# Cosine attention and a low-rank mixer on one core: the second half of batch 0's residual goes through a DMA transpose instead of TensorE

## The chip, the cores and the metric

The kernel runs on one core of one Trainium2 chip. The metric is the time of one execution in device microseconds (us); less is better. Five runs of the kernel before the change gave 579.52 to 582.07 us, with a median of 579.97 us.

## What is computed

There are 8 batches, 12 heads, 448 positions and 64 values per head, so that a position has 768 channels. The mixer adds a low-rank mix over positions and then a two-layer network with 3072 hidden units and a residual:

```python
attn = softmax((q/|q|) @ (k/|k|).T / tau) @ v          # per batch and head
x    = attn with heads side by side                    # 8 x 448 x 768
u    = x + (x.T @ U @ V).T                             # U: 448x32, V: 32x448
out  = u + relu(u @ w_ch1) @ w_ch2                     # 768 -> 3072 -> 768
```

The change concerns the `u +` of the last line, for half of the channels of one batch.

## The kernel before

**The tiles.** Two heads make a pair, so each batch has six pairs, numbered 0 to 47 over the whole kernel; pairs 6 to 11 are batch 1. `u` is kept transposed: `uE` (even batches) and `uO` (odd ones) are tiles of 128 partitions by six blocks of 512 columns, with channels on the partitions and positions along the columns. The mixer's first layer (`steps_m1`, line 513) makes 24 tiles of 128 hidden units, each from six matmuls, one for every block of `u`; ScalarE or VectorE applies the ReLU (lines 517 and 519). The second layer (`steps_m2`, line 540) works by chunks of 128 positions and 384 channels: 24 matmuls add up in one PSUM tile `mp`, whose pool has two buffers. Batch 0 has three chunks for each half of the channels.

**The residual.** The output has positions on the partitions, so `u` must be turned back before it is added. For batch 0 TensorE does this: behind the 24 matmuls of a chunk, three more (line 550) multiply blocks of `uE` by the identity into the same `mp`, and then ScalarE (line 554) or VectorE (line 556) copies `mp` into the output tile `o_sb`. Which of the two takes the copy is decided while the program is built, by running totals of each engine's estimated time (`est.act_first`). For all later batches `turn(b, half)` (line 500) issues one DMA transpose of three blocks of `u` into a tile `ut`, and VectorE reads both `mp` and `ut` and adds them into `o_sb` (line 558). The pool of `ut` has two buffers, one of which is held by the raw matrix V until `place_copies` has read it.

**The order of the work.** Everything is issued in an order written out by hand; each engine works through its own list in order and waits on semaphores. Steps of the mixer of batch b-1 are pulled from a list named `fill` between the attention steps of batch b. `put(n, i, fn)` hooks an extra step behind the i-th attention step of pair n. The stage around the change is that of pairs 10 to 14, some 84 to 125 us into the span, where the second layer of batch 0 ends and the first layer of batch 1 begins. What it issues, in order:

- pair 11: scores of pair 11; then `step_V` for both halves of pair 10 (lines 376, 383) with the divisions on VectorE (lines 394, 395), and the DMA transpose `XT` of pair 10 (`step_XT`, line 461).
- pair 12: scores (lines 331, 324); both halves of `step_V` of pair 11 and its `XT`; `step_A2` (line 469), whose matmuls read the `X` tiles of pairs 10 and 11.
- pair 13: scores; `step_H2` (line 483), after which two VectorE adds (line 488) put together blocks 4 and 5 of `uO` from PSUM and the `XT` tiles of pairs 10 and 11, and one VectorE copy (line 491) takes over the last 64 positions of `uE`; then the rest of `fill` and the start of batch 1's first layer.
- pair 14: `step_S3` (line 343) reads the `qkT` tiles of pairs 14 and 15, which come by DMA transposes (`step_T`, line 315).

**The transfer queue.** Nearly all DMAs are issued by SyncE (SP), in one list: loads of q, k and v (lines 205 to 214), the transposes `qkT`, `XT` and `ut`, and the stores of `o_sb` (lines 564, 568). A DMA in that list waits, if need be, for the data that it reads and for the DMA eight places ahead of it in the list, whose semaphore it shares. The second layer's weights come by GpSimd's queue (line 173).

The instructions of TensorE that read what VectorE wrote, in the stage of pair 13, have separate waits: the first matmul of batch 1's first layer waits for a free `mp`; only the fifth and sixth, which read blocks 4 and 5 of `uO`, wait for the two adds of line 488; the seventh, which begins the second tile, waits for the `mp` of batch 0's last chunk to be read.

Of the kernel before, what the change touches and what calls it, by code (L numbers as in the profile page):

```python
# [22 lines left out]
def kernel(  # L23
# [23 lines left out]
    NP = H // 2  # L47
    CC = C // 128
    NC = F // 128
# [360 lines left out]
    def u_of(b):  # L410
        return uE if b % 2 == 0 else uO
# [82 lines left out]
    ut_of = {}  # L494

    def turn(b, half):

        t = work.tile([128, 3, 4, 128], BF, name="ut", tag="ut", bufs=2)
        ut_of[(b, half)] = t
        nc.sync.dma_start_transpose(  # L500
            out=t.rearrange("p k c d -> p (k c) d"),
            in_=u_of(b)[:, 3 * half:3 * half + 3, :].rearrange("p k s -> p (k s)"))
# [22 lines left out]
    def steps_m2(b):  # L525
        u = u_of(b)
        if b % 2 == 0:
            chunks = [(64 + 128 * c, 128 * c, c) for c in range(3)]
        else:
            chunks = [(384, 384, 3)] + [(128 * c, 128 * c, c) for c in range(3)]  # L530
        steps = []
        state = {}

        def part(half, ci, lo, hi, c0=0, c1=HC):
            r0, u0, c = chunks[ci]
            if lo == 0:
                state["mp"] = psum.tile([128, HC], FP, name="mp", tag="ps_m", bufs=2)
            mp = state["mp"][:, c0:c1]
            for f in range(lo, hi):
                nc.tensor.matmul(out=mp, lhsT=relu[:, f, r0:r0 + 128],  # L540
                                 rhs=w2_sb[:, f, half * HC + c0:half * HC + c1],
                                 start=(f == 0), stop=(b > 0 and f == NC - 1), skip_group_check=True)
            est.pe(0.0004 * (c1 - c0 + 6) * (hi - lo))
            if hi < NC:
                return
            o = work.tile([128, HC], FP, name="o_sb", tag="o_sb", bufs=3)[:, c0:c1]
            if b == 0:
                for i in range(3):
                    cc = half * 3 + i
                    nc.tensor.matmul(out=mp[:, i * 128:(i + 1) * 128], lhsT=u[:, cc, u0:u0 + 128],  # L550
                                     rhs=ident, start=False, stop=(i == 2), skip_group_check=True)
                est.pe(0.17)
                if est.act_first(0.48, 0.55):
                    nc.scalar.copy(out=o, in_=mp)
                else:
                    nc.vector.tensor_copy(out=o, in_=mp)
            else:
                nc.vector.tensor_add(o.rearrange("p (k d) -> p k d", d=128),  # L558
                                     mp.rearrange("p (k d) -> p k d", d=128),
                                     ut_of[(b, half)][:, c0 // 128:c1 // 128, c, :])  # L560
                est.dve(0.55)
            cols = slice(half * HC + c0, half * HC + c1)
            t4 = out[b, 0:256, cols].rearrange("(p c) d -> c p d", c=4)
            nc.sync.dma_start(out=t4[c], in_=o[0:64, :])
            if c < 3:
                t3 = out[b, 256:448, cols].rearrange("(p c) d -> c p d", c=3)
                other = nc.scalar if b == B - 1 and half == 1 else nc.sync
                other.dma_start(out=t3[c], in_=o[64:128, :])
            else:
                t4e = out[b - 1, 0:256, cols].rearrange("(p c) d -> c p d", c=4)  # L570
                nc.sync.dma_start(out=t4e[3], in_=o[64:128, :])

        for half in range(2):
            for ci in range(len(chunks)):
                if (b, half, ci) == (B - 1, 1, len(chunks) - 1):

                    for cs in ((0, 256), (256, 384)):
                        for i in range(2):
                            steps.append(lambda half=half, ci=ci, i=i, cs=cs:
                                         part(half, ci, 12 * i, 12 * i + 12, *cs))  # L580
                    continue
                for i in range(4):
                    steps.append(lambda half=half, ci=ci, i=i: part(half, ci, 6 * i, 6 * i + 6))
        return steps
# [150 lines left out]
    def put(n, at, fn):  # L735
        after.setdefault((n, at), []).append(fn)
# [42 lines left out]
    put(NP + 1, 2, lambda: (load_w2(1, 0, 12), load_w2(1, 12, 24)))  # L779
    put(NP + 2, 2, load_copies)  # L780
    put(NP + 5, 5, place_copies)

    def spread(n, order, nf, first=0):

        weights = [w if fn is not False else 0 for w, fn in order]
        given = acc = 0
        for i, ((_, fn), w) in enumerate(zip(order, weights)):
            if fn:
                fn()
            for g in after.pop((n, i + first), []):  # L790
                g()
            acc += w
            want = nf * acc // sum(weights)
            f(min(want - given, len(fill)))
            given = want

    KEEP = 3
    for n in range(NP, NPAIR + 1):
        b, p = pairs[n] if n < NPAIR else (B, 0)
# [116 lines left out]
```

## Time and profile before

| | us |
|---|---|
| median of 5 runs | 579.97 |
| lowest and highest run | 579.52, 582.07 |
| the profiled execution, its own time | 579.97 |
| its span | 578.1 |
| time around the span | 1.9 |
| TensorE busy | 568.3 (98% of the span) |
| ScalarE busy | 262.1 (45%) |
| GpSimd busy | 214.0 (37%) |
| VectorE busy | 212.1 (37%) |

The profile is one execution. Its views give, for each line and engine, how often an instruction ran and how long it took; for each stretch of time what every engine did, in order; who waited for whom; for each DMA how long its issue took on the issuing engine's queue (`SPq`) and how long it was from there until the data had landed; and the chain of waits, which is followed back from the last instruction to whatever released it. All times of instructions below are counted from the start of the span. TensorE's matmuls overlap each other, so the step from one start to the next says what a matmul costs, and not its duration.

### The profile page before, as it was taken

Reading aid. Unit: us, or ns where it says so; the run is one execution under the profiler, and the core shown is the slowest. Engines: PE = TensorE matmul, PEld = TensorE weight load, DVE = VectorE, ACT = ScalarE, POOL = GpSimd, SP = SyncE. Lnnn points to the kernel's source line nnn. Section 1 sums busy time; section 2 is a strip of 40 time slices with the busy share of each in tenths; the row PEclk is TensorE's granted clock in tenths of the full one; section 3 lists DMA queues with packets and bytes.
Section 4 is the critical chain, followed back from the end, with each engine's and each line's share of the span. In section 5 each row is a group of like instructions: output and inputs, shape, how many; then the busy total and the mean of one; then the engine's idle time right before and its main releaser. Section 6 shows DMA issues by size and latency. Waiting matters only on the chain.

```text
span 578.1 us, 12301 instructions
## 1 busy us (share of the span) xinstructions
PE 568.3 (98%) x5098; PEld 328.7 (57%) x5098; DVE 212.1 (37%) x460; ACT 262.1 (45%) x449; POOL 214.0 (37%) x202
## 2 busy tenths in 40 slices
PE   6999999999999999999999999999999999999997
PEld 6665566555565555555555555655555555655565
DVE  6874551433342334423324343432244332320011
ACT  4877544455423653446324555246433374214300
POOL 8756574715416236416055064253261420000000
PEclk9999999999999999999999999999999999999999
DMA  6899999686477376576365664773755640231022
GB/s 163 190 241 236 237 209 215 166 167 138 105 148 168 85 146 131 133 147 110 88 155 148 118 137 97 150 174 81 131 130 114 132 74 15 55 70 37 6 50 57
DMA packets 139881, 74.52 MB, mean 129 GB/s; under 512 B 86688, under 2 KB 139696, under 8 KB 139824
## 3 DMA queue, kind: packets, MB, share of 16 engines
q1 hardware_dynamic: 129568, 63.20, 50.7%
q0 software_dynamic: 9632, 10.01, 10.2%
q8 instruction: 40, 0.66, 0.5%
q10 hardware_dynamic: 624, 0.51, 0.3%
q14 instruction: 17, 0.14, 0.1%
HBM read 52.19 MB, written 11.01 MB: 109 GB/s over the span
## 4 chain that ended last, share of the span: by engine, by line
PE 88%; DMA 7%; DVE 1%; SPq 1%; ACT 1%; POOL 1%; issue 0%; DVEq 0%; POOLq 0%; ACTq 0%
PE mp L540 38%; PE mp L513 33%; PE sc L331 5%; DMA w_sb<-in_moe_w_ch_dram 5%; PE av L383 3%; PE up L383 2%; DMA kst<-in_k_dram 1%; PE av L376 1%; PE av L343 1%; PE up L376 1%; PE up L469 1%; DMA qst<-in_q_dram 1%; PE av L483 1%; PE tp L300 0%; ACT E L356 0%
## 5 line engine op out<-in xcount | busy, mean ns | idle before, releaser
L540 PE MATMUL mp<-w_sb,relu 128*128 128x384 bf16 (+2 forms) x1368 | 233.7, 323 | 0.3 <-DMA w_sb<-in_moe_w_ch_dram 0.3
L540 PEld LDWEIGHTS <-relu 128*128 128x128 bf16 x1368 | 126.8, 98 | 88.8 <-issue 13.4
L513 PEld LDWEIGHTS <-w_sb 128*128 128x128 bf16 x1128 | 105.1, 98 | 99.1 <-issue 9.3
L517 ACT ACTIVATE relu<-mp 128x448 bf16<-128x448 f32 x163 | 88.7, 544 | 128.2 <-PE mp L513 128.2
L356 ACT ACTIVATE E<-sc 128x896 bf16<-128x896 f32 x144 | 125.1, 922 | 21.9 <-PE sc L331 20.8
L268 POOL TENSOR_TENSOR qk<-kst,inv 128x512 bf16<-128x512 f32 x43 | 46.0, 1070 | 236.0 <-DVE inv L262 228.9
L513 PE MATMUL mp<-uO,w_sb 128*128 128x448 bf16 x576 | 114.2, 352 | 0.0
L513 PE MATMUL mp<-uE,w_sb 128*128 128x448 bf16 x552 | 112.9, 353 | 0.0
L558 DVE TENSOR_TENSOR o_sb<-mp,ut 128x384 f32<-128x384 f32 (+2 forms) x51 | 28.0, 550 | 141.0 <-PE mp L540 141.0
L248 DVE TENSOR_REDUCE ss<-sq 128x16 f32<-128x1024 f32 (+1 forms) x50 | 57.6, 1165 | 1.8 <-ACT sq L240 1.1
L268 POOL TENSOR_TENSOR qk<-qst,inv 128x512 bf16<-128x512 f32 x44 | 47.4, 1079 | 1.0 <-PE up L441 1.0
L383 PEld LDWEIGHTS <-E 128*128 128x128 bf16 x1152 | 45.0, 97 | 0.0
L519 DVE TENSOR_SCALAR relu<-mp 128x448 bf16<-128x448 f32 x25 | 15.6, 625 | 76.3 <-PE mp L513 75.8
L243 POOL TENSOR_TENSOR sq<-kst 128x1024 f32<-128x1024 f32 (+1 forms) x23 | 42.7, 1858 | 0.8 <-ACT E L353 0.6
L331 PE MATMUL sc<-qkT 64*64 64x448 bf16 x576 | 42.4, 359 | 0.6 <-ACT E L356 0.3
L243 POOL TENSOR_TENSOR sq<-qst 128x1024 f32<-128x1024 f32 x21 | 39.8, 1894 | 6.7 <-DMA qst<-in_q_dram 5.8
L353 ACT ACTIVATE E<-av 128x448 bf16<-128x448 f32 x17 | 9.2, 541 | 47.3 <-PE up L343 47.3
L276 POOL CAST v<-vst 128x1024 bf16<-128x1024 f32 (+1 forms) x25 | 25.2, 1007 | 13.9 <-DMA vst<-in_v_dram 11.5
L383 PE MATMUL av<-v,E 128*128 128x65 bf16 x624 | 28.0, 193 | 0.0
L394 DVE RECIPROCAL rd<-av 128x4 f32<-128x4 f32 x52 | 9.3, 179 | 47.3 <-PE av L383 47.3
L473 ACT CAST A_sb<-up 128x128 bf16<-128x128 f32 x19 | 5.0, 264 | 47.6 <-PE up L469 47.6
L376 PEld LDWEIGHTS <-E 128*128 128x128 bf16 x192 | 18.0, 98 | 14.5 <-issue 0.8
(97 smaller groups left out, 346.8 us busy)
## 6 DMA issues: line engine op xcount, KB each, us to landing
out_dram<-o_sb SPq DMA_DIRECT2D x108, 96.0 KB, 2.3
w_sb<-in_moe_w_ch_dram POOLq DMA_DIRECT2D x8, 1152.0 KB, 18.3
qst<-in_q_dram SPq DMA_DIRECT2D x23, 256.0 KB, 3.9
vst<-in_v_dram SPq DMA_DIRECT2D x46, 128.0 KB, 3.1
kst<-in_k_dram SPq DMA_DIRECT2D x44, 128.0 KB, 2.8
qst<-in_q_dram SPq DMA_DIRECT2D x23, 192.0 KB, 4.0
vst<-in_v_dram SPq DMA_DIRECT2D x46, 96.0 KB, 2.9
kst<-in_k_dram SPq DMA_DIRECT2D x44, 96.0 KB, 2.9
```

Source lines behind the costliest of these rows:

```text
L243: nc.gpsimd.tensor_mul(sq[:, 0:self.nh * 4, :], self.flat(t), self.flat(t))
L248: nc.vector.reduce_sum(self.ss[:, j, 0:self.nh * 4], self.sq[j][:, 0:self.nh * 4, :], axis=AX.X)
L268: eng.tensor_mul(qks[self.gi % 2][:, j, i, :, :, :], t[:, 2 * j:2 * j + 2, :, :].rearrange("p h c d -> p c h d"), iv.unsqueeze(3).to_broad ...
L276: nc.gpsimd.tensor_copy(out=self.flat(v65[self.s])[:, :, 0:D], in_=self.flat(vst[self.s]))
L331: nc.tensor.matmul(out=sc[o:o + 64, h, 0:S], lhsT=t[r, 1, c * 128 + o:c * 128 + o + 64], rhs=t[r, 0, 0:S], start=True, stop=True)
L356: nc.scalar.activation(out=e[:, 2 * c:2 * c + 2, 0:S], in_=sc[:, :, 0:S], func=AF.Exp)
L376: nc.tensor.matmul(out=av[:, i, :, :], lhsT=last_of(b, p)[:, ic * 128:(ic + 1) * 128], rhs=vv[:, 2 * j:2 * j + 2, 3, :], start=(i == 0), s ...
L383: nc.tensor.matmul(out=av[:, i, h, :], lhsT=e[:, 2 * c + h, ic * 128:(ic + 1) * 128], rhs=vv[:, 2 * j + h, c, :], start=False, stop=(i == ...
L513: nc.tensor.matmul(out=mp, lhsT=w1_sb[:, cc, f * 128:(f + 1) * 128], rhs=u[:, cc, 0:S], start=(cc == 0), stop=(cc == CC - 1))
L517: nc.scalar.activation(out=relu[:, f, o:o + S], in_=mp, func=AF.Relu)
L540: nc.tensor.matmul(out=mp, lhsT=relu[:, f, r0:r0 + 128], rhs=w2_sb[:, f, half * HC + c0:half * HC + c1], start=(f == 0), stop=(b > 0 and f ...
L558: nc.vector.tensor_add(o.rearrange("p (k d) -> p k d", d=128), mp.rearrange("p (k d) -> p k d", d=128), ut_of[(b, half)][:, c0 // 128:c1 / ...
```

## The change

`turn(0, 1)` is hooked behind step 2 of pair 11, that is, behind the scores and ahead of the second half of `step_V` of pair 10. It issues the DMA transpose of blocks 3 to 5 of `uE`, which hold the second half of batch 0's channels. The second layer asks whether a turned tile exists for its half, and not whether the batch is 0. So the three chunks of the second half lose the nine identity matmuls and the three copies, and get three additions on VectorE; the first half stays as it was. Two of the three copies were ScalarE's and one was VectorE's.

```diff
             mp = state["mp"][:, c0:c1]
+            turned = (b, half) in ut_of
             for f in range(lo, hi):
                 nc.tensor.matmul(out=mp, lhsT=relu[:, f, r0:r0 + 128],
                                  rhs=w2_sb[:, f, half * HC + c0:half * HC + c1],
-                                 start=(f == 0), stop=(b > 0 and f == NC - 1), skip_group_check=True)
+                                 start=(f == 0), stop=(turned and f == NC - 1), skip_group_check=True)
...
-            if b == 0:
+            if not turned:
                 for i in range(3):
                     cc = half * 3 + i
                     nc.tensor.matmul(out=mp[:, i * 128:(i + 1) * 128], lhsT=u[:, cc, u0:u0 + 128],
                                      rhs=ident, start=False, stop=(i == 2), skip_group_check=True)
...
     put(NP + 5, 5, place_copies)
+    put(NP + 5, 2, lambda: turn(0, 1))
```

In the lists of instructions that the two programs build to, the rest is the same on every engine: TensorE's has the nine matmuls and their weight loads less, ScalarE's has two copies less, VectorE's has three additions in place of one copy, GpSimd's is unchanged, and SP's has one transpose more, directly ahead of `XT` of pair 10. On VectorE the first addition stands between the divisions of the two halves of pair 11, the second where the copy stood, and the third behind the copy of line 491.

## The prediction

> **What bounds the kernel.** I read the page's busy shares first, then the chain of waits, to see whether any engine but TensorE sets the end.
>
> ```profile
> PE 568.3 (98%) x5098; PEld 328.7 (57%) x5098; DVE 212.1 (37%) x460; ACT 262.1 (45%) x449; POOL 214.0 (37%) x202
> ...
> PE 88%; DMA 7%; DVE 1%; SPq 1%; ACT 1%; POOL 1%; issue 0%; DVEq 0%; POOLq 0%; ACTq 0%
> ```
>
> TensorE is busy for 98% of the span and makes 88% of the chain; the rest of the chain lies ahead of the first mixer steps. From 80 to 135 us, where the change is, the chain runs on TensorE alone. So whatever TensorE no longer does there is gained, and whatever it newly waits for is lost, and neither is given back later: in the list of waits, TensorE's matmuls wait for nothing from 84 us to the end. What the other engines do counts only where TensorE comes to wait for it. The chain around the three chunks (start, us on the chain):
>
> ```profile
> 100.14 0.17 PE mp L550 x3
> 100.30 0.12 PE up L376 x2
> ...
> 103.91 0.23 PE up L469 x8
> ...
> 105.72 0.17 PE mp L550 x3
> ...
> 110.59 0.17 PE mp L550 x3
> 110.76 2.27 PE mp L513 x12
> ```
>
> Each group of three identity matmuls holds 0.17 us of the chain. Next I read SP's own timeline (start, duration of the issue), since the new transpose goes into that list.
>
> ```profile
> 97.18 0.60 SPq L214 DMA_DIRECT2D kst<-in_k_dram  x1
> 97.88 1.23 SPq L461 DMA_TRANSPOSE XT<-X  x1
> 99.15 0.60 SPq L211 DMA_DIRECT2D vst<-in_v_dram  x1
> ...
> 103.03 0.65 SPq L205 DMA_DIRECT2D qst<-in_q_dram  x1
> 103.73 1.84 SPq L206 DMA_DIRECT2D qst<-in_q_dram  x1
> 105.66 0.56 SPq L564 DMA_DIRECT2D out_dram<-o_sb  x1
> 106.27 0.59 SPq L568 DMA_DIRECT2D out_dram<-o_sb  x1
> 106.96 1.25 SPq L461 DMA_TRANSPOSE XT<-X  x1
> ```
>
> The reader is to see that SP has no hole here: each issue begins 0.04 to 0.1 us behind the end of the one before, from 93.10 to 126.48 us. The `XT` of pair 11 (106.96) is issued 5.5 us after VectorE has written its `X` (101.05 + 0.43), only because the list ahead of it takes that long. A DMA put in at 97.88 therefore moves all that follow by its whole issue time. The last view is VectorE's timeline, which says who needs that `XT`:
>
> ```profile
> 100.84 0.18 DVE L394 RECIPROCAL rd<-up 128x4 f32<-128x4 f32 x1 [1.00 <-PE up L383]
> 101.05 0.43 DVE L395 TENSOR_TENSOR X<-up,rd 128x256 bf16<-128x256 f32 x1
> ...
> 109.49 0.62 DVE L488 TENSOR_TENSOR uO<-up,XT 128x448 bf16<-128x448 f32 x1 [1.27 <-DMA XT<-X]
> 110.03 0.62 DVE L491 COPY uO<-uE 128x384 bf16<-128x384 bf16 x1
> ```
>
> VectorE already waits 1.27 us for this `XT` (issued 106.96, landing 2.4, used 0.13 later), and TensorE needs the result soon after, at the sixth matmul of batch 1's first layer.
>
> **Removed.** Nine matmuls in three groups: 3 x 0.17 = 0.51 us off TensorE's path. Two ScalarE copies of 0.48 us and one VectorE copy of 0.56 us go too; ScalarE has holes of 1 to 2 us around them, so they are worth nothing by themselves.
>
> **Added on SP.** One `ut` transpose ahead of `XT` of pair 10. The rows of the other fourteen:
>
> ```profile
> L500 SPq DMA_TRANSPOSE ut<-uO x8: 1393/1484/2210, 120.3 to 519.1; - x8
> L500 SPq DMA_TRANSPOSE ut<-uE x6: 1363/1520/1987, 185.4 to 469.9; - x6
> ...
> DMA to landing us min/median/max: 3.7/3.9/4.8
> ```
>
> Issue: 1.46 us (the middle of the rows) and 0.05 us to the next, so d = 1.51 us; bounds 1.41 and 2.26 from the shortest and longest row. One thing can lower d: the issue of 1.84 us at 103.73 is 1.22 us longer than its line's median of 0.62. If that is a wait whose end does not move, it swallows 1.22 of d and leaves 0.3. Such long issues turn up every ten to twenty DMAs all along SP's timeline whatever is issued, so I take it as moving along; one more of them in the stretch would make d 2.7.
>
> **Added on VectorE, route A: the first addition.** It waits for `ut`, and the division of pair 11's second half, two reductions and the next additions stand behind it on VectorE. Who waits for that division is `step_A2` on TensorE, at 103.84 before, 0.17 us earlier now. The `ut` is issued at 97.88. Its landing is 3.9 us in the median, but here the DMA engines are full (mean share over 1.1 in every stretch of 1 us from 97.5 to 101.5): the `XT` issued at that very place landed after 3.9 us against 2.4 in the median of its kind. I add the same 1.5 us: 5.4 us, landing at 103.28. Bounds: 3.7 from the shortest `ut`, and 6.8 from the slowest `qkT` transpose (issued at 87.39, still beside the weight load). Then the addition starts 0.13 us later and holds VectorE for 0.56, and the division takes 0.64 (100.84 to 101.48), so `X` is there 1.33 us behind the landing and TensorE goes on some 0.05 later, at 104.66. That is 0.82 us later than before. The next two groups are gone as well, so at 110.59 the shift by this route is 0.82 - 0.34 = +0.48 us. In general it is the landing time less 4.92 us, and never under -0.51.
>
> **Added on VectorE, route B: the third addition.** It stands behind the add of line 488 that waits for `XT` of pair 11, and that `XT` comes later by d. VectorE: add at 109.49 + d, the copy of line 491 0.54 later, the addition 0.55 later again, its end 0.56 later: 111.14 + d. This addition frees the `mp` that the second tile of batch 1's first layer needs; before, ScalarE's copy freed it at 110.79 + 0.48 = 111.27. The second tile starts six matmuls (6 x 0.19) behind 110.59, at 111.72, so before it had 0.45 us to spare. Now it starts at 111.19 + d, a shift of d - 0.53 = **+0.98 us**. The sixth matmul itself wants 109.49 + d + 0.62 = 111.62 and is reached at 112.03 by route A, so it adds nothing.
>
> **The sum.** The two routes meet at the same matmuls and the later one counts: max(-0.51, 0.48, 0.98) = +0.98 us, in which the 0.51 us are already contained. Some of the lag between engines is modelled, and the chain puts the start of the first layer 0.17 us later than the timeline does, which gives +0.81; I take +0.9.
>
> **What else moves with SP's list.** `qkT` of pair 15 landed at 117.6 + 3.1 = 120.7 and is read at 122.08; moved by d it lands at 122.2, against 122.98 for a TensorE that is itself 0.9 us late: free, by 0.8 us. The v load that GpSimd casts at 104.34 comes 1.5 us later and the cast ends near 107, before the scaling that starts at 107.44 or later. SP's first hole follows there (1.5 us ahead of the `XT` at 128.04), and the delay ends in it. The DMA engines have shares near 0.6 from 102 on, so the additional transfer slows nobody beyond that.
>
> **Two rules weighed.** The row says that a turn of twelve 128x128 blocks lands in 3.7 to 4.8 us. The Trainium skill, "VectorE: DVE Perf Modes", section "The three transpose paths", speaks against this change: it gives 390 ns for a TensorE transpose and 1309 ns for one by DMA, and says to use TensorE wherever a PSUM destination will do. Read as a price per block, an estimate from that page is 12 x 1.31 = 15.7 us for a turn and a stall of some 11 us by route A; the rows here are four times shorter, so the measurement decides. The row also says that an issue holds SP for 0.6 us, and 1.4 to 2.2 for a turn. "DMA: Bandwidth & Descriptors", section "Issuing engines are not separate DMA queues", calls the time to initiate a DMA usually small against the DMA; with d near nothing route B would be gone and the sum would be +0.48 by route A alone. In this stretch SP is full, so the rows speak against that.
>
> **Rivals.** *The gain comes whole* (579.5 us, -0.51): it needs d under 0.02 and a landing under 4.4 us. For it: five of the fourteen turns landed in 3.7 or 3.8 us, and the long issue at 103.73 may swallow most of d. Against it: SP's full list and the slow `XT` at the same place. A half of it, d = 0.3 with the landing at 5.4, gives +0.48. *Slower beyond what can be told from no change* (582 us): one mechanism, SP's delay on `XT` of pair 11. It decides from d = 2.27, where d - 0.53 passes 1.74 us. With the longest turn (2.26) it gives +1.73; with one more long issue (d = 2.7) +2.2, or 582.2 us. For it: the turn at 120.25 also followed transposes and took 2.21 us. Against it: eleven of the fourteen took 1.36 to 1.56. A landing of 6.8 us by route A would give +1.88 and end at the same place. *The change does nothing*: excluded, since the built list has all nine matmuls less and the additions are in place.
>
> **How the numbers follow.** The profiled execution took 579.97 us, 1.87 more than its span of 578.1, and happens to be the median of the five runs too. So the forecast is 579.97 + 0.9 = 580.9 us. Chances: forecast (+0.3 to +1.6) 0.55; gain whole or nearly (-0.51 to 0) 0.15; half of it (0 to +0.3) 0.1; slower rival 0.2. About 0.3%, 1.74 us, is what a measurement of this kernel can tell from no change. The gain is bounded by 0.51 us, so faster by more than that is only a mishap of measuring, 0.02; slower is the last rival, 0.2; the rest, 0.78, is within. The range goes from the whole gain, 579.5, to the slower rival's end, 582.2.
>
> **What would show it.** In the changed profile: nine instead of eighteen identity matmuls, three groups gone from the chain (-0.51); the `ut` issued at about 97.9 with an issue near 1.5 and a landing near 5.4; the first addition waiting on it, and TensorE waiting for `X` at `step_A2` by about 0.8 us; `XT` of pair 11 issued near 108.5; the second tile of batch 1's first layer starting near 112.7, released by the third addition. I am wrong if SP's list has caught up at 108.5 without a hole, or if TensorE waits at `step_S3`.

## The result and the profile after

| | us |
|---|---|
| changed kernel, median of 30 runs | 582.13 (579.74 to 585.0) |
| kernel before, 51 runs beside them | 579.94 (579.36 to 582.07) |
| ratio, 95% interval | 1.0033 [1.0024, 1.0042] |
| profiled execution, its own time and span | 579.99, 578.2 |

The changed kernel is slower by 2.2 us by the medians (1.4 to 2.4 us by the interval of the ratio). The profiled execution is not: it stands 0.02 us above that of before. In part that is chance: it enters the stage of the change 0.33 us earlier (VectorE's division of pair 11's first half starts at 98.87 instead of 99.20); ahead of it TensorE does not wait for weights, as it did for 0.3 us before. The 30 runs lie in three groups: nine from 579.7 to 581.0, thirteen from 581.4 to 582.6 and eight from 583.5 to 585.0. So the profile of after shows one of the short executions, and what makes the others long had to be found in further profiles.

The busy times and the shares of the chain that ended last, on the page of after:

```profile
PE 569.1 (98%) x5089; PEld 329.4 (57%) x5089; DVE 212.7 (37%) x462; ACT 261.2 (45%) x447; POOL 214.1 (37%) x202
...
PE 92%; SPq 2%; DMA 2%; DVE 2%; ACT 1%; issue 1%; DVEq 0%; ACTq 0%
```

Nine matmuls and two ScalarE copies are gone and VectorE has two instructions more, as the diff says. The chain now holds DMA, SP and VectorE inside the mixer. In the rows of the changed kernel, lines behind the diff's first new line are counted one higher (558 is L559, 540 is L541; in e9 and e10 below, one more from line 492 on). The pieces of the chain around the three chunks (start, us on the chain):

```profile
97.49 4.73 DMA ut<-uE
...
102.30 0.56 DVE o_sb L559
...
103.46 0.30 PE up L469 x8
...
107.61 2.89 DMA XT<-X
...
110.59 0.12 DVE uO L488
...
111.14 0.25 DVE uO L491
111.39 0.48 DVE o_sb L559
111.86 0.04 issue
111.91 1.29 PE mp L513 x6
```

The chain goes over the `ut` transpose, the first addition and the division to `step_A2` (route A), and then over `XT` of pair 11, the add of line 488, the copy of line 491 and the third addition to the second tile of batch 1's first layer (route B). In between, TensorE sets it for 3.6 us. The chain also puts 0.55 us of the first add of line 488 there, but that add held nothing up: SP issues `XT` 0.10 us behind the end of the issue before it (107.51), the same gap as before (106.86 to 106.96). SP's timeline (start, duration of the issue):

```profile
97.49 1.36 SPq L500 DMA_TRANSPOSE ut<-uE  x1
98.95 1.68 SPq L461 DMA_TRANSPOSE XT<-X  x1
...
105.26 0.96 SPq L206 DMA_DIRECT2D qst<-in_q_dram  x1
...
107.61 1.23 SPq L461 DMA_TRANSPOSE XT<-X  x1
```

From the new slot to `XT` of pair 11 it is now 10.12 us, against 9.08 before (97.88 to 106.96). So d, the time by which the turn sets SP's list back, is 1.04 us here: the turn's 1.46 with its gap, 0.45 more for the `XT` behind it, and 0.88 less for the long issue of line 206, with what is left in the gaps.

### The profile page after: what moved, and what is told of

Its sections match the earlier page's. It is cut to its first block, busy times and chain, and to the rows that moved or that the text cites. A ratio compares the mean times of both kernels' runs of the same rounds, so it can differ in the third digit from the quotient of the medians.

```text
span 578.2 us, 12282 instructions
## 1 busy us (share of the span) xinstructions
PE 569.1 (98%) x5089; PEld 329.4 (57%) x5089; DVE 212.7 (37%) x462; ACT 261.2 (45%) x447; POOL 214.1 (37%) x202
## 4 chain that ended last, share of the span: by engine, by line
PE 92%; SPq 2%; DMA 2%; DVE 2%; ACT 1%; issue 1%; DVEq 0%; ACTq 0%
PE mp L513 37%; PE mp L541 36%; PE sc L331 6%; PE av L383 3%; PE up L383 2%; PE av L376 1%; PE av L343 1%; PE tp L300 1%; DMA ut<-uE 1%; PE sc L656 1%; PE up L469 1%; PE up L376 1%; DMA qst<-in_q_dram 1%; PE av L483 1%; DMA XT<-X 1%
## 5 line engine op out<-in xcount | busy, mean ns | idle before, releaser
L541 PE MATMUL mp<-w_sb,relu 128*128 128x384 bf16 (+2 forms) x1368 | 233.5, 323 | 0.0
L541 PEld LDWEIGHTS <-relu 128*128 128x128 bf16 x1368 | 126.9, 98 | 88.5 <-issue 13.1
L559 DVE TENSOR_TENSOR o_sb<-mp,ut 128x384 f32<-128x384 f32 (+2 forms) x54 | 29.7, 550 | 143.8 <-PE mp L541 141.0
```

Source lines behind the costliest of these rows:

```text
L541: nc.tensor.matmul(out=mp, lhsT=relu[:, f, r0:r0 + 128], rhs=w2_sb[:, f, half * HC + c0:half * HC + c1], start=(f == 0), stop=(turned and ...
```

## The experiments

Four theories stood after the result. **A**: the first addition waits for `ut` and holds the division that `step_A2` needs. **B**: SP's delay of `XT` holds the third addition, which frees the `mp` of the second tile. **C**: the `qkT` transposes of pair 15, also set back on SP, hold `step_S3`. **D**: the copy of line 491, between the add of line 488 and the third addition, is far longer than 0.55 us in some executions, when it comes to lie beside another instruction of GpSimd than before. All ratios are to the kernel before, in runs beside it on the same chip (its medians there are 579.70 to 579.85).

**The changed kernel again, three times (e1, e1b, e1c).** No edit.

> The changed kernel as it is, once more, for a second profile: the thirty runs of it lie between 579.7 and 585.0 us, while the profiled one took 579.99 and so is among the shortest. Theory A (the first addition waits for the turned tile and holds back the division that step A2 needs): a longer execution shows TensorE waiting ahead of A2 at about 103.5 us by the excess over 580. Theory B (SP's list delays XT of pair 11 and with it the third addition): it waits at 110 to 113 us, at the sixth matmul and the second tile of batch 1's first layer. Theory C: at step_S3, near 122 us.

> The changed kernel as it is, timed beside the three that follow on one chip. The second profile gave 580.16 us, again among the shortest of the thirty runs (median 582.1), so the profiles have not shown the longer executions yet. If the difference lay in the chip, the median here would be near 580.3; if it lies in the kernel, near 582 with a spread of some 5 us. A profile of a longer execution would show by theory A a late landing of the turned tile and TensorE waiting at A2, by theory B a late XT of pair 11.

> The changed kernel as it is, as the control beside the two that follow. The third profile (582.16 us) showed what a longer execution does: the XT of pair 11 lands late as in theory B, and then VectorE's copy of line 491, which stands ahead of the third addition, takes 1.52 us in place of 0.25 to 0.62, ending 0.12 us behind a GpSimd square that began 0.5 us ahead of it. Theory D: that copy waits until the GpSimd instruction that is running has ended; whether it meets a short one, a square of 1.9 us or the gap between them is a matter of some tenths of a us, and this makes two kinds of execution about 2 us apart. Expected here: 580 to 584, as before.

Measured: e1 580.16 (one run, again a short one); e1b 580.82, ratio 1.0026 [1.0009, 1.0043]; e1c 583.09, ratio 1.0049 [1.0034, 1.0064]. So the groups have other shares in each series. The profile of e1b is of an execution of 582.16 us, so one of the middle group. Its timelines where after had 111.91 (start, duration, what the engine waited for before):

```profile
104.94 1.63 SPq L205 DMA_DIRECT2D qst<-in_q_dram  x1
...
108.66 1.25 SPq L461 DMA_TRANSPOSE XT<-X  x1
...
111.40 0.62 DVE L488 TENSOR_TENSOR uO<-up,XT 128x448 bf16<-128x448 f32 x1 [3.40 <-PE mp L513]
111.45 1.89 POOL L243 TENSOR_TENSOR sq<-qst 128x1024 f32<-128x1024 f32 x1
111.94 1.52 DVE L491 COPY uO<-uE 128x384 bf16<-128x384 bf16 x1
113.39 0.54 DVE L559 TENSOR_TENSOR o_sb<-mp,ut 128x384 f32<-128x384 f32 x1
113.98 1.29 PE L513 MATMUL mp<-uO,w_sb 128*128 128x448 bf16 x6 [1.55 <-DVE o_sb L559]
```

The first VectorE row names TensorE as what ended its wait, but the chain of e1b goes over the transpose there, which landed at 111.31:

```profile
108.66 2.65 DMA XT<-X
```

GpSimd's square (line 243) runs from 111.45 to 113.34. The copy starts at 111.94 and ends at 113.46, just behind it. In after the copy started 0.02 us ahead of the same square; it took 0.25, and the square 1.98 instead of 1.89:

```profile
111.14 0.25 DVE L491 COPY uO<-uE 128x384 bf16<-128x384 bf16 x1
111.16 1.98 POOL L243 TENSOR_TENSOR sq<-qst 128x1024 f32<-128x1024 f32 x1
```

The copy of the same 128x384 tile so costs 0.25 or 1.52 us, and TensorE pays the difference: 1.55 us of waiting at the second tile, against 0.28. This is what formed theory D. e1c shows it again, and its second tile waits 1.89 us:

```profile
113.05 1.89 POOL L243 TENSOR_TENSOR sq<-qst 128x1024 f32<-128x1024 f32 x1
113.20 1.86 DVE L491 COPY uO<-uE 128x384 bf16<-128x384 bf16 x1
```

**The turn two pairs earlier, in the weight load (e2).**

```diff
-    put(NP + 5, 2, lambda: turn(0, 1))
+    put(NP + 3, 2, lambda: turn(0, 1))
```

> The same transpose, issued some 30 us earlier, in the hole of SP's list between 68 and 83 us, by hooking it behind step 2 of pair 9. Nothing else changes. If the loss is the place in SP's list and the late landing (A and B), both go, the 0.51 us of the nine matmuls stay gained: 579.4 us with a spread like that of the kernel before (about 579.4 to 582). If the loss is the additions on VectorE by themselves, or the extra 0.4 MB of traffic, it stays at about 582.

Measured: 583.15, ratio 1.0056 [1.0036, 1.0076]. From SP's timeline of this kernel, and its list of TensorE's waits from 70 to 130 us (us in total, times, longest):

```profile
67.90 6.46 SPq L500 DMA_TRANSPOSE ut<-uE  x1
```

```profile
PE mp L541 <- DMA w_sb<-in_moe_w_ch_dram: 3.2, 1, 3.2
```

Neither A nor B is there any more: no other wait is listed, and SP reaches `XT` of pair 11 without the turn. But beside the load of the weights the turn's issue takes 6.46 us and its landing 16.2, and TensorE waits 3.2 us for weights, where it waited 0.3 before. The cost has moved, and grown, and the 579.4 us that were expected did not come. This does not tell A from B.

**The first chunk by TensorE again (e3)** (three identity matmuls back, the first addition gone).

```diff
-            turned = (b, half) in ut_of
+            turned = (b, half) in ut_of and b + ci > 0
```

> The transpose is issued where the change issues it, but the first of the three chunks still gets its residual from TensorE (three identity matmuls and a ScalarE copy), so no instruction waits for the turned tile before about 105.5 us. Theory A: the loss goes, 579.7 to 580.2 us and a narrow spread. Theory B: the loss stays, 581.5 to 582.5.

Measured: 581.03, ratio 1.0016 [1.0007, 1.0025]. Route A is cut off, and the kernel is still slower than before. In its profile (580.56 us) the sixth matmul waits 0.5 us for the add of line 488 and the second tile 0.3 for the third addition. So A is not needed for a loss; B is there without it. But the median lies under the 581.5 us that B had foreseen, and the highest run is 581.52: the long executions are gone too. In the profile the copy of line 491 starts at 111.68, 0.12 us ahead of the square, and takes 0.28 us; that it passes ahead of the square in the other runs as well is inferred.

**The turn issued, its tile not read (e4)** (all three chunks by TensorE).

```diff
-            turned = (b, half) in ut_of
+            turned = b > 0
```

> The transpose is issued where the change issues it, but nothing reads it: all three chunks keep TensorE's residual and the copies, as in the kernel before. What is left is the DMA and its 1.5 us in SP's list. Theory A: 580.0, as before. Theory B in the form of the prediction needs the third addition to be late; here ScalarE frees that tile, so only the sixth matmul can wait, by up to 0.3 us: 580.0 to 580.4. Theory C, or contention among the DMAs: 581.5 or more.

Measured: 579.96, ratio 1.0003 [0.9993, 1.0012]. SP's delay and the transfer alone cost nothing that shows in the time, though the sixth matmul waits 0.36 us for the add of line 488. The profile holds a copy of the long kind as well:

```profile
111.53 1.90 POOL L243 TENSOR_TENSOR sq<-qst 128x1024 f32<-128x1024 f32 x1
111.55 1.99 DVE L491 COPY uO<-uE 128x384 bf16<-128x384 bf16 x1
```

Here 1.99 us harm nobody, since ScalarE and not VectorE frees the `mp`. The loss needs both: the late `XT`, and the third addition behind it on VectorE.

**`XT` of pair 11 ahead of the q load (e5).**

```diff
-                  2 * NP + 4: [(m - 4, i) for i in (0, 2, 4)]}
+                  2 * NP + 4: [(m - 4, i) for i in (2, 2, 4)]}
```

> The two loads of q for pairs 16 and 17, which SP issues ahead of the XT of pair 11, are put behind it; their reader on GpSimd has time. So XT of pair 11 is issued about 1.5 to 2.5 us earlier. The first addition still waits for the turned tile. Theory B: the third addition is in time, the profile shows no wait at the second tile of batch 1's first layer, and the time falls by 0.7 to 1.1 us against the changed kernel. Theory A: the long executions stay, median 581 to 582 with a wide spread.

Measured: 579.33, ratio 0.9993 [0.9985, 1.0002]; e1b, the changed kernel on the same chip, has 1.0026. From its timelines:

```profile
106.12 1.22 SPq L461 DMA_TRANSPOSE XT<-X  x1
...
109.22 1.03 DVE L491 COPY uO<-uE 128x384 bf16<-128x384 bf16 x1
110.17 0.54 DVE L559 TENSOR_TENSOR o_sb<-mp,ut 128x384 f32<-128x384 f32 x1
```

The two loads that stood ahead of `XT` now follow it; it is issued 1.49 us earlier than in after, and TensorE waits for nothing between 84 and 140 us. Batch 1's first layer starts at 109.85, against 110.59 before. With B gone the loss is gone, by 1.5 us of the medians, where 0.7 to 1.1 had been expected. The edit also sets GpSimd's square back, which reads these loads (it starts at 111.95, behind the copy), so e5 does not show the late `XT` by itself. Whether a gain is left (0.4 us by the medians) is not settled, since the interval holds 1.

**The same, with the first chunk by TensorE (e6)** (e5's edit and e3's).

> Both edits: q loads behind XT of pair 11, and the first chunk's residual by TensorE. Nothing of A or B is left, and six of the nine matmuls stay away (-0.34): 579.5 to 579.7 us if A and B are all there is. If it is above 580.3, a third cost has been overlooked.

Measured: 580.16, ratio 1.0008 [0.9996, 1.0020]. It is not better than e5, though 579.5 to 579.7 had been expected, so nothing points to the first addition as a cost worth removing. In its profile a store's issue of 1.74 us at 103.56 set `XT` back to 107.31, and the second tile waited 0.33 us again.

**The same, with the first addition later (e8).** e5's edit; the addition of the first chunk and its stores are kept back until the third quarter of the next chunk, behind the division of pair 11 and the first reduction.

```diff
+            if (b, half, ci, lo) == (0, 1, 1, 12):
+                state["late"]()
...
+            if (b, half, ci) == (0, 1, 0):
+                state["late"] = lambda: finish(half, c, mp, o, c0, c1, True)
```

> All nine matmuls stay away. VectorE's first addition is moved behind the division of pair 11's second half and the first reduction, so that a late tile holds back neither; q loads behind XT of pair 11. If A is the division standing behind the waiting addition and B the delay of that XT, both are gone and the gain is whole: 579.3 to 579.6 us. If A is something else that a late tile does, the time stays above 580.

Measured: 579.74, ratio 0.9994 [0.9986, 1.0003]: as e5 within the intervals, and over the 579.6 that was expected. In the profiled execution (581.54 us) TensorE waits 0.6 us at `step_S3` for the last `qkT`: theory C, where B and A are gone. It also waited 0.9 us for weights ahead of the stage.

**The copy of line 491 on ScalarE (e9)** (for batch 1 only).

```diff
-            nc.vector.tensor_copy(out=uO[:, :, S:512], in_=uE[:, :, 384:S])
+            copy = nc.scalar.copy if b == 1 else nc.vector.tensor_copy
+            copy(out=uO[:, :, S:512], in_=uE[:, :, 384:S])
```

> For this batch the copy of line 491 is made by ScalarE instead of VectorE; all else is as in the changed kernel, the late XT too. Theory D (the copy waits for GpSimd, the third addition for the copy): the third addition follows at once on the add of line 488, the executions of 582 us and more vanish, median 579.8 to 580.3 us. Theory B alone (only the late XT): the copy was worth 0.5 us, so the median falls by 0.5 us against the control and the spread of 4 to 5 us stays.

Measured: 580.29, ratio 1.0007 [0.9998, 1.0017], highest run 581.43; e1c, the changed kernel on the same chip, has a median of 583.09 and a lowest run of 581.94. The two kernels' runs do not overlap. TensorE in its profile (581.43 us, the longest of its runs):

```profile
112.89 1.76 PE L514 MATMUL mp<-uO,w_sb 128*128 128x448 bf16 x7 [1.26 <-DVE uO L488]
```

What is left is the wait for the late `XT` (issued at 109.33, since the load of line 205 took 2.00 us there). With the copy off VectorE the third addition follows 0.54 us behind the add (112.21). The row holds the sixth matmul and the second tile together; the chain shows that the tile still waits for that addition, 0.46 us behind the sixth matmul instead of 0.19:

```profile
112.75 0.56 DVE o_sb L560
113.31 0.04 issue
113.35 1.29 PE mp L514 x6
```

**The squares of GpSimd later (e11)** (out of this stage; the copy stays on VectorE).

```diff
+        if m == 2 * NP + 4:
+            at[0:2] = [(m - 2, -1), (m - 2, -1)]
```

> VectorE's list is that of the changed kernel, the copy of line 491 stays ahead of the third addition, and XT comes as late. Only GpSimd's two squares for pairs 16 and 17 are put behind its next cast, which waits for a load until 116 to 117 us, so that GpSimd runs nothing from about 111.3 us on. Theory D: the copy takes 0.25 us whenever it starts behind the last scaling, the long executions vanish, median 579.9 to 580.4 us. If the copy is slow for another reason (DMA traffic, ScalarE), it still takes up to 2 us in some executions and the median stays at 581 to 582.

Measured: 580.62, ratio 1.0010 [1.0000, 1.0019], highest run 581.41, on the chip of e1c and e9. From its timeline:

```profile
110.67 0.25 DVE L491 COPY uO<-uE 128x384 bf16<-128x384 bf16 x1
110.83 0.55 DVE L559 TENSOR_TENSOR o_sb<-mp,ut 128x384 f32<-128x384 f32 x1
...
115.98 1.04 POOL L276 CAST v<-vst 128x1024 bf16<-128x1024 f32 x1 [5.22 <-DMA vst<-in_v_dram]
```

The copy starts 0.10 us ahead of the end of GpSimd's last scaling (109.71 + 1.06), takes 0.25 us, and no long execution is left, though the median is 0.2 us over the range expected. Two edits that share nothing but the pair of copy and square, one moving the copy and one the square, do the same, so D is confirmed.

**`XT` first and the copy on ScalarE (e10)** (e5's edit and e9's).

> The version that the experiments point to: the turn where the change puts it, all nine matmuls away, the two q loads behind XT of pair 11, and this batch's copy of line 491 on ScalarE. Nothing is left for TensorE to wait for in this stage, so the gain should be whole: 579.2 to 579.5 us, and the few executions above 580.4 that the run with only the q loads moved still had (two of twelve) should go if they came from that copy; if they stay, they come from elsewhere, as they do in the kernel before.

Measured: 580.20, ratio 1.0008 [0.9999, 1.0017]; the 579.2 to 579.5 us that were expected did not come, and it is not better than e5 (which ran on another chip). TensorE at `step_S3` in its profile (581.41 us):

```profile
122.53 0.38 PE L343 MATMUL av<-qkT 64*64 64x448 bf16 x2
123.59 0.38 PE L343 MATMUL up<-qkT 64*64 64x448 bf16 x2 [0.68 <-DMA qkT<-qk]
```

This is C once more: take B and D away, and the `qkT` of pair 15 is the next transfer on SP's list to be late. No kernel here beats the one before by more than its interval.

## Why the prediction came out as it did

One instruction decides: the start of the second tile of batch 1's first layer. Set beside each profiled execution's own time (us; "entered" is the start of the division of pair 11's first half, which stands ahead of all that the change touches, to before; "step" is from the start of the copy to the start of the third addition):

| profile | entered | `XT` issued | add of line 488 | step | second tile, to before | own time, to before |
|---|---|---|---|---|---|---|
| before | 99.20 | 106.96 | 109.49 | - | 111.72 | 579.97 |
| after | -0.33 | 107.61 | 110.59 | 0.16 | +0.19 | +0.02 |
| e1 | -0.39 | 107.94 | 110.49 | 0.37 | +0.28 | +0.19 |
| e1b | +0.04 | 108.66 | 111.40 | 1.45 | +2.26 | +2.19 |
| e11 | -0.62 | 107.27 | 110.12 | 0.16 | -0.28 | -0.45 |
| e5 | -0.36 | 106.12 | 108.67 | 0.95 | -0.74 | -0.71 |
| e9 | +0.32 | 109.33 | 112.21 | none | +1.63 | +1.46 |

Where tiles follow without a wait, the second is taken at 0.189 us a matmul. The two last columns agree within 0.2 us, in e2, e3, e4 and e6 too, so in these executions nothing after that tile gives time back or takes more. In e1c, e8 and e10 something does: the clock in the first, `step_S3` in the others. What happens ahead of the change differs from execution to execution ("entered"); without it the second tile is 0.52 us late in after, 0.67 in e1 and 2.22 in e1b. The 0.98 us of the prediction lie between the short and the long ones.

**Removed, right.** Nine matmuls are gone, 0.51 us. e8, where no late tile holds TensorE ahead of the first layer, shows it unspoilt: it enters the stage 1.25 us later than before and starts the first layer 0.75 later (111.34), so 0.50 us are gained in between. e5 enters 0.36 us earlier and starts 0.74 earlier; of the gain 0.38 are left, since route A holds TensorE there.

**Route A, mechanism right, size wrong.** The first addition does wait for `ut` (2.79 us of VectorE's time), and the division behind it. But the turn landed in 4.73 us, where the prediction took 5.4, and `step_A2` began (103.46) about 0.12 us later than TensorE could have begun it, instead of 0.99. So the first layer started 0.39 us early, counted from the entry into the stage, and not 0.48 late. The 1.5 us added for full DMA engines were too much; the median of the rows, 3.9, was too little.

**Route B, right as the one that decides.** All its links are in the chain of after. Three terms of its sum, "d - 0.53", differ. d was put at 1.51; it was 1.04 in after and 1.07 in e11, where the long load issue shrank to 0.96 and 0.97, 1.42 in e1 (1.32), and 1.70 in e1c, 1.71 in e1b and 2.08 in e9, where it fell on line 205 and took 1.55, 1.63 and 2.00. So the long issue, which the prediction took as moving along unchanged, did not. From issue to add it took 2.55 to 2.98 us, not 2.53. And the step from copy to addition, "the addition 0.55 later again", is the one that failed.

**The term that was mis-sized: the step over the copy, 0.55 us.** It was taken from one row (0.62), beside which GpSimd was in a scaling of 1.06 us. It measured 0.16 in after and e11, 0.37 in e1, 1.45 in e1b and 1.78 in e1c: the copy takes at least 0.25 us, and ends 0.1 us behind the GpSimd instruction that is running when it starts if that is later. The profile of before has this already, in its later batches: a copy that starts in a square ends 0.1 us behind it, and one with GpSimd idle takes 0.25:

```profile
243.03 1.89 POOL L243 TENSOR_TENSOR sq<-qst 128x1024 f32<-128x1024 f32 x1
...
244.57 0.46 DVE L491 COPY uO<-uE 128x384 bf16<-128x384 bf16 x1
...
514.98 0.25 DVE L491 COPY uO<-uE 128x384 bf16<-128x384 bf16 x1
```

So the four copies of that line, read beside GpSimd's list, would have given the price. The late `XT` moves the copy from 110.03, among the scalings, to 111.0 and later, where squares of 1.9 us begin. With the measured terms the sum is right: after 0.65 + 0.45 - 0.39 - 0.53 = +0.18 (measured +0.19); e1b 1.70 + 0.21 + 0.90 - 0.53 = +2.28 (measured +2.26). It comes within 0.02 us for e1, e1c and e11 as well, and for e9 with a step of 0. The terms are the issue of `XT`, the way from there to the add, the step less 0.55, and the old 0.53.

The Trainium skill, "SBUF — State Buffer", section "Who interferes with whom", has the rule that I did not apply: VectorE's copies between SBUF tiles, in their fast modes, use a port pair that GpSimd needs, whichever issues first holds it for its whole instruction, and the other is blocked. The runs agree: 0.25 us with GpSimd idle (514.98 in before), 1.52 to 1.99 when a square of 1.9 had just begun, and the square 1.98 instead of 1.89 when the copy came first.

**The rivals.** The forecast was +0.9 us and the medians gave +2.2. The slower rival named 582.2 us, and the median came out at 582.13, 0.07 inside the range, but for another reason than the one given, and that is luck: the rival wanted d at or over 2.27, and e9 with 2.08, the largest d seen, cost +1.46, while e1b with 1.71 cost +2.19. Not SP's delay alone carries an execution past 1.74 us, but the copy that it drops behind a square. The whole gain needed d under 0.02 and never came by this kernel.

**What else was to move.** "Free, by 0.8 us" held for the `qkT` of pair 15 while TensorE itself was late. In e5, where it is early, the tile lands at 121.5 us and is read at 121.53, with nothing to spare; in e8 and e10 TensorE waits 0.6 and 0.7 us there. Not foreseen at all was the clock. In e1c, where TensorE waited 0.59 and 1.89 us with one matmul in between, it then ran at half clock for a while (columns: window, PE, PEld, DVE, ACT and POOL busy, granted clock, DMA share, GB/s):

```profile
110.00:115.00 5.00, 3.10 (x18) 1.56 (x16) 2.34 (x3) 0.72 (x2) 4.95 (x5) 1.00 0.64 165
115.00:120.00 5.00, 4.42 (x27) 2.42 (x27) 1.14 (x4) 0.54 (x1) 2.44 (x2) 0.66 0.73 207
```

The windows of 1 us from 117 to 119 show a clock of 0.50, those from 116 and from 119 show 0.70 and 0.59. A mean of 0.66 over 5 us is then 3.4 us at 0.5, and an estimate from that is a cost of 1.7. That execution took 585.3 us, 5.33 more than before: +3.86 at the second tile (1.50 of it by entering the stage late, behind a wait of 1.4 us for weights) and 1.47 after it, for which the clock is enough. Of the 30 runs of the changed kernel, the six from 583.65 up have mean clocks of 0.994 to 0.997 against 0.999 to 1.0 for the rest; that they lost it at the same place is inferred, since only e1c has a profile. What makes the other two of the longest group, at the full clock, is not known.

So the late `XT` alone leaves a loss of 0.5 (e9) to 0.8 us (e11) when the long copies are gone, by the medians on a chip where the changed kernel itself costs 3.3 us (e1c); the rest goes with the copy behind the square, and with the half clock that its wait brings on in some runs. The 2.2 us of the first series, whose median lies in the middle group, are the same two costs by this account, but their shares were not measured there. Open are why SP's issues of line 205 or 206 take 0.65 us at one time and up to 2.0 at another (which decides how late `XT` is, and so into which group an execution falls), why the groups' shares differ between the series, and whether e5's 0.4 us are a gain.

## What to carry to other kernels

Before putting a transfer into a queue without holes, follow each later transfer to the instruction that waits for it, and then every instruction behind that one on its engine: what frees the next buffer may stand there. Read the duration of each of these instructions together with what the other engines run at the same moment; one row is no price for an instruction that another engine can hold up. Where a kernel's times lie in groups, a profile of the fastest one does not explain the others; take profiles until one of each group is there.

## What the runs showed of the hardware

- A copy of 128x384 bf16 by VectorE inside SBUF took 0.25 us with GpSimd idle and up to 1.99 beside a GpSimd square of 1.9. The wait is part of the instruction's duration and no idle time, so no list of waits shows it. It is not the copy alone: line 260 on VectorE (128x32 f32), 0.18 us in before, took 0.89 in e6, ending 0.03 us behind a cast of GpSimd:

```profile
106.55 1.04 POOL L276 CAST v<-vst 128x1024 bf16<-128x1024 f32 x1 [3.27 <-DMA vst<-in_v_dram]
106.73 0.89 DVE L260 TENSOR_SCALAR ss<-ss 128x32 f32<-128x32 f32 x1 [0.42 <-ACT ss L254]
```

- Half a clock for 3.4 us followed waits of 0.59 and 1.89 us (e1c), and none followed waits of 0.77 and 1.55 (e1b). The Trainium skill, "TensorE: Matmul & The Clock Gate", section "What's actually happening", puts the half clock behind at least one idle window of about 3.4 us; no single gap here was longer than 1.89, so here it came on with less.
- A DMA transpose of twelve 128x128 blocks, 1.36 us to issue and 4.7 to land at 97 us, took 6.46 and 16.2 us when issued beside the weight load at 68 us (e2).
